# Batch 0's turns, squares and begun FFN1 pieces in another order; the last product's two column groups in one tile

## The chip, the cores and the metric

The kernel runs on one core of one Trainium2 chip. The metric is the device time of one execution in microseconds (us), as the median of several runs. One more execution is taken with the hardware profiler; its trace is where the times of single instructions come from.

A core has engines that each work through their own queue of instructions in a fixed order: TensorE (PE in the profile; its weight loads are PEld), VectorE (DVE), ScalarE (ACT), GpSimd (POOL) and SyncE (SP). They wait for each other through semaphores. Data moves between the off-chip memory and the on-chip memory by DMA transfers, which SP, ACT or POOL issue. TensorE writes its results to PSUM, eight banks of 2 KB for each of 128 partitions, and VectorE or ScalarE copy them out.

## The reference

Attention without a softmax, then a two-layer FFN with a parametric relu between the layers, on 8 batches, 12 heads, 448 positions and a head dimension of 64:

```
S = 448; scale = 1 / sqrt(64)
scores = scale * (q @ k.T)                    # per batch and head, 448 x 448
attn   = max(scores, 0) ** 2 / S
x      = (attn @ v), heads side by side       # 3584 x 768
h      = x @ w_in                             # 3584 x 2048
g      = max(h, 0) + alpha * min(h, 0)
out    = g @ w_out                            # 3584 x 768, float32
```

## The kernel before

**Work and stages.** The 12 heads of a batch form 3 groups of 4 heads, so there are 24 groups n in all; groups 0 to 2 belong to batch 0. A group's 448 positions are 64 rows (pp) by 7 columns (j), and a piece (n, j) of the scores is called a chunk here: four matmuls on quarters of the array (`score_mm`, L209), one relu over 128x896 on ScalarE or VectorE (`relu`, L218 or L220), one square (`square`, L229 or L231). After seven chunks `attnv` multiplies by v (28 matmuls, L241) and copies the result out, scaled, into xT, which is FFN1's input (L253, L255). FFN1 of a batch is 16 blocks `ff` of 128 columns, each of six matmuls over `km` (`f1_mm`, L275) and the parametric relu (`f1_out`, L281 on ScalarE and L282 on VectorE). FFN2 multiplies two token blocks at a time by w_out in seven products instead of eight (class `Pair`, L335 and L340), except for some blocks done directly (`f2`, L300). `store` (L291) sends a finished tile out in two transfers of 64 rows each.

**Turning q and k.** The scores need q and k with the head dimension on the partitions. For groups 0 to 4 TensorE does that (`turn_pe`, L183): two transposes per j into PSUM, then a copy to the tile T (L186) on VectorE or ScalarE. For the later groups a DMA transpose does it. For group 0, q is loaded in two parts in float32 and cast (`cast0`, L406), and k in two parts, j 0 to 3 and j 4 to 6.

**An order written by hand.** The order of all work is a text of words that `Walk.step` carries out one by one; each engine's queue follows from it. The words that matter here:

- `t0q24D`: group 0, q, transposes for j 2 and 3, copied by VectorE (D) or ScalarE (A). `x02D` is the cast of j 0 and 1.
- `i6`: six matmuls on an idle tile (`warm`, L165); 31 such stand at the very start.
- `cA`, `cD`: the next chunk's scores, and its relu on ScalarE or VectorE. `cAA` is two of them.
- `s1D`: the square of the chunk that is second in the list `late` of relued chunks, on VectorE.
- `v`: `attnv` of the next group; the letters behind it name the engines of the two halves of its copy (AD if none is given).
- `e4`: the next four matmuls of FFN1 pieces that are begun early: four blocks `ff`, each over `km` 0 to 3 (groups 0 and 1), 16 matmuls in all, in banks that are held. `E` completes one of them with `km` 4 and 5, once group 2 is in xT, and runs `f1_out`.
- `Lq3`, `Lv3`, `Li1`, `Lo0,0,8`: loads of q and k, of v, of w_in columns and of w_out, issued on POOL's queue in the order of the text.
- `r4e`, `r4x`, `r4y`: the last of the seven products of the last `Pair`, in two column groups (0 to 255 and 256 to 383).

The text of the first `walk` call (L502) carries batch 0's attention up to the first four FFN1 blocks. `LAST` (L514) carries the last batch's FFN. The word `z` in it makes `store` use ScalarE's queue for the second transfer of each tile, beside SP's.

**Tiles that are passed on.** The relu writes into one of six `rl` buffers, which the square reads and gives back; an instruction that needs a buffer waits for the one that reads it last. PSUM banks are handed out by `take_pair` and `take_bank`, the one longest unused first.

Of the kernel before, what the change touches and what calls it, by code (L numbers as in the profile page):

```python
# [20 lines left out]
def kernel(  # L21
# [11 lines left out]
    B, H, S, D = q.shape  # L33
# [465 lines left out]
                nc.vector.tensor_scalar(beta_sb, alpha_sb, -1.0, 1.0, ALU.mult, ALU.add)  # L499

    walk = Walk()
    walk("""Li0 Lv2 x02D x46A x24D x67A i6 t0q46D t0q24A t0q67A t0q02D t0k01D t0k24D t0k12A cA cD Lq3 cA Li1 t0k47D cA s1D t1q07D cAA s0D Li2 Lq4 s0D t1k07D cA s2D s1D Li3 cAA s0D s0D cA cDA t2q07D s1D t2k05D cA s0D Lo0,0,8 s2D Lq5 Lv3 t2k57A Lo0,8 s0D Lv4 s0D cA cA cA Lv5 s0D s0D v cA v cA s0A cD e4 e1 s0D cD s0D cA s1A s1A e5 e4 e1 s0D e1 s0D v b t3q07A t3k07D E E E E""")  # L502
    walk("""f f cADA f s0D f s1D s0D cADA f t4q07A t4k07D m o f s0D f cAAA s0D s1D d5D f f s0D f l5 Lq6 f Lq7 Lq8 g00 Lo1,0,4 s0D cADA s2D vDA cDD s3D s0D s0A g20 s0A g10 s0D cADA v s0D cAA s0D s1D s0D s0D""")
    walk("""B h h cAA h s0D s0D h v d6D l6 Lo1,4 Lv6 h E E E d7D f E f E f f d8D f l8 cAAA s1D f Lq9 f Lv7 s1A Lq10 Lv8 f f f s0D f""")
    walk.p, walk.r = Pair((0, 3), (0, 4)), Pair((0, 5), (0, 6))
# [5 lines left out]
    FIRST_PAIR = """B f s1A f s2D s0D s1D n f f s0D f f f f s0D cDA cA f s0D s1A nD pa pb r1 f pc s0A f f f f f f p6 r2 cADA s1D v cAA ra s0D pd cA p7 rb n p5 s2D p4 s0D p3 s1A s0A cADA s2A s0D rc r6 v rd cADA s2D r7 r5 s0A s0D cAAD s0A r4 r3 cA v cAA"""  # L511
    EACH = """B f s0D f s0A f n f f f f s2A f s1D cAAA s1D f f s0D f s0A f p1 nD f f r1 f f s1A pc p2 pa r2 ra pb cA vDA s1D s0D cAA p6 s0D pd p7 n cA rc s1A cAA s0D s0A p5 p4 rb p3 cAAD v cAD s1D s1A s3A cA s3A r6 s2A r7 rd r5 s0A cAD r4 s0D r3 cAD v cD cA"""
    ONE_PAIR = """B f f nD s2A s0A s2D f s1D f f f s1D f f s0A f f cAD s1D cA s0D n s0D f f f f f f pc pa g50 pb cADA v p1 cAAA s0A p6 s2D s0A p2 pd p7 s1A p5 n s0A p4 p3 s0D cADA s0D v cAD s1A s2A cD s2A s1D g51 s0D cDAD v cD cA cA"""
    LAST = """B f s0A f f f f s3A s2A s2A f f s2A f f f f f f pc f f s0A f p1 r1 pa pb p2 p6 p7 pd ra p5 rb rc p4 p3 r6 z r7 rd r5 r2 r3 r4e"""  # L514
    for b, plan in ((2, FIRST_PAIR), (3, EACH), (4, EACH), (5, ONE_PAIR), (6, EACH), (7, LAST)):
        walk.p, walk.r = ([walk.r] if b == 2 else []) + [Pair(*t) for t in pairs[b][b == 2:]] + [None] * (b == 5)
        walk(plan)
# [30 lines left out]
```

## Time and profile before

| what | value |
|---|---|
| median of 3 runs | 372.95 us (372.71, 372.95, 373.54) |
| the profiled execution, its own time | 373.66 us |
| its span, first to last instruction | 371.9 us |
| mean granted TensorE clock | 0.995 |
| VectorE, ScalarE busy | 277.9 us (75%), 274.7 us (74%) |
| chain that ended last: PE, ACT, DVE | 91%, 3%, 2% |

The span begins at 0; all places in the profile are us from there. The page gives each engine's busy time, then 40 equal slices of about 9.3 us, one digit each (9 is 90% or more busy; for PEclk, the granted share of TensorE's clock in tenths). A window's row gives the busy time of each engine in that stretch, with the number of instructions, the granted clock and the load of the DMA engines. A timeline row gives start, length, engine, line, operation, output and input, how often it follows itself, and in brackets the idle time of the engine before it and what ended it. A "released by" is inferred from semaphore events.

### The profile page before, as it was taken

The page shows a single profiled execution, that of the slowest core. Times are in us where ns is not written, and L with a number is a line of the kernel's source. Part 1 is how long each engine was busy: PE and PEld are TensorE (multiplying, and loading weights), DVE is VectorE, ACT ScalarE, POOL GpSimd, SP SyncE. Part 2 cuts the span into 40 slices and gives each one's busy share as a digit, 9 for nine tenths or more (in the row PEclk, how much of TensorE's full clock was granted, in tenths as well). Part 3 has the DMA queues.
Part 4 walks back from the last instruction along what each step waited for, and adds up shares of the span by engine and source line. Part 5 has one row for each costly group of instructions (what it writes and reads, how often), then busy time and mean ns, then how long its engine had stood idle before and what let it go on. Part 6 is the DMA issues. An engine that isn't in the chain of part 4 may idle for free.

```text
span 371.9 us, 7878 instructions
## 1 busy us (share of the span) xinstructions
PE 362.9 (98%) x3097; PEld 196.7 (53%) x3097; DVE 277.9 (75%) x445; ACT 274.7 (74%) x406; POOL 72.5 (19%) x120
## 2 busy tenths in 40 slices
PE   7799999999999999999999999999999999999996
PEld 5454564445454565545555455554555455555563
DVE  3989988885968989566887668888849667856653
ACT  4998676877997678885897859967699866964400
POOL 8567150304113222021020220202200000000000
PEclk9899999999999999999999999999999999999999
DMA  9999979998999878455882558727647201220024
GB/s 145 193 204 202 196 120 187 159 167 148 183 173 141 119 118 156 102 85 92 156 150 64 96 81 167 143 59 121 101 95 136 50 2 43 65 65 0 0 64 108
DMA packets 73557, 43.29 MB, mean 116 GB/s; under 512 B 40368, under 2 KB 73008, under 8 KB 73520
## 3 DMA queue, kind: packets, MB, share of 16 engines
q0 software_dynamic: 27136, 22.58, 42.0%
q1 hardware_dynamic: 45712, 19.61, 26.1%
q10 hardware_dynamic: 672, 0.59, 0.5%
q8 instruction: 24, 0.39, 0.4%
q14 instruction: 13, 0.11, 0.1%
HBM read 45.62 MB, written 11.01 MB: 152 GB/s over the span
## 4 chain that ended last, share of the span: by engine, by line
PE 91%; ACT 3%; DVE 2%; DMA 1%; issue 1%; ACTq 0%; DVEq 0%; POOLq 0%
PE psum L275 38%; PE psum L335 30%; PE psum L209 8%; PE psum L241 8%; PE psum L300 6%; DMA kraw<-in_k_dram 1%; ACT rl L218 1%; PE psum L183 1%; DVE gT L282 1%; ACT xT L253 1%; ACT neg L281 1%; DVE w_mix L195 1%; DVE at L231 0%; DVE T L186 0%; DVE osb L340 0%
## 5 line engine op out<-in xcount | busy, mean ns | idle before, releaser
L275 PE MATMUL psum<-xT,w_in_sb 128*128 128x448 bf16 x768 | 150.4, 353 | 0.3 <-DVE gT L282 0.2
L282 DVE SCALAR_TENSOR_TENSOR gT<-neg,beta_sb,psum 128x448 bf16<-128x448 f32 x128 | 85.2, 679 | 43.4 <-ACT neg L281 42.1
L218 ACT ACTIVATE rl<-psum 128x896 bf16<-128x896 f32 x128 | 111.1, 924 | 7.2 <-PE psum L209 5.2
L275 PEld LDWEIGHTS <-w_in_sb 128*128 128x128 bf16 x768 | 73.4, 98 | 73.2 <-issue 6.7
L281 ACT ACTIVATE neg<-psum 128x448 f32<-128x448 f32 x128 | 68.5, 547 | 41.0 <-PE psum L275 32.7
L231 DVE TENSOR_TENSOR at<-rl 128x896 bf16<-128x896 bf16 x105 | 62.1, 618 | 0.5 <-ACT rl L218 0.2
L229 ACT ACTIVATE at<-rl 128x896 bf16<-128x896 bf16 x63 | 58.5, 951 | 0.3
L335 PEld LDWEIGHTS <-S 128*128 128x128 bf16 x384 | 36.7, 98 | 28.4 <-issue 5.3
L335 PE MATMUL psum<-w_mix,S 128*128 128x384 bf16 x288 | 49.8, 326 | 0.2
L220 DVE TENSOR_SCALAR rl<-psum 128x896 bf16<-128x896 f32 x40 | 43.2, 1086 | 8.6 <-PE psum L209 8.1
L209 PE MATMUL psum<-T 64*64 64x448 bf16 x672 | 46.2, 361 | 2.1 <-DVE T L186 1.3
L418 POOL COPY landed<-T 1x1 bf16<-1x1 bf16 x18 | 4.1, 229 | 206.8 <-DMA T<-perm 183.1
L335 PEld LDWEIGHTS <-gT 128*128 128x128 bf16 x296 | 28.3, 98 | 20.2 <-issue 1.8
L241 PE MATMUL psum<-at,vraw 64*64 64x448 bf16 x672 | 36.5, 350 | 0.0
L335 PE MATMUL psum<-w_out_sb,gT 128*128 128x384 bf16 x192 | 34.0, 326 | 0.0
L340 DVE TENSOR_TENSOR osb<-psum,u 128x384 f32<-128x384 f32 (+2 forms) x37 | 20.2, 546 | 12.6 <-PE psum L335 8.2
L209 PEld LDWEIGHTS <-T 64*64 64x64 bf16 x672 | 17.4, 106 | 23.1 <-issue 14.9
L241 PEld LDWEIGHTS <-vraw 64*64 64x64 bf16 x672 | 21.2, 107 | 11.8 <-issue 2.7
L300 PE MATMUL psum<-w_out_sb,gT 128*128 128x256 bf16 (+1 forms) x128 | 22.0, 326 | 0.1
L255 DVE TENSOR_SCALAR xT<-psum 128x448 bf16<-128x448 f32 x24 | 14.9, 622 | 9.2 <-PE psum L241 8.7
L253 ACT ACTIVATE xT<-psum 128x448 bf16<-128x448 f32 x24 | 13.2, 549 | 9.1 <-PE psum L241 8.7
L356 ACT COPY osb<-psum 128x384 f32<-128x384 f32 x12 | 5.8, 479 | 17.4 <-PE psum L335 17.4
(43 smaller groups left out, 239.8 us busy)
## 6 DMA issues: line engine op xcount, KB each, us to landing
out_dram<-osb SPq DMA_DIRECT2D x91, 96.0 KB, 2.3
vraw<-in_v_dram POOLq DMA_DIRECT2D x24, 224.0 KB, 6.6
qraw<-in_q_dram POOLq DMA_DIRECT2D x23, 224.0 KB, 4.1
kraw<-in_k_dram POOLq DMA_DIRECT2D x23, 224.0 KB, 5.3
w_in_sb<-in_moe_w_in_dram POOLq DMA_DIRECT2D x16, 192.0 KB, 8.1
w_out_sb<-in_moe_w_out_dram POOLq DMA_DIRECT2D x4, 512.0 KB, 10.5
w_out_sb<-in_moe_w_out_dram POOLq DMA_DIRECT2D x4, 256.0 KB, 8.8
out_dram<-osb SPq DMA_DIRECT2D x8, 128.0 KB, 3.6
```

The lines of the kernel that those rows point to most:

```text
L209: nc.tensor.matmul(ps[64 * c:64 * c + 64, r, :S], t[64 * r:64 * r + 64, 1, j, 64 * c:64 * c + 64], t[64 * r:64 * r + 64, 0, :, 64 * c:64 * ...
L218: nc.scalar.activation(rl, ps[:, :, :S], ACTF.Relu)
L220: nc.vector.tensor_scalar(rl, ps[:, :, :S], 0.0, None, ALU.max)
L229: nc.scalar.activation(a, rl, ACTF.Square)
L231: nc.vector.tensor_tensor(a, rl, rl, ALU.mult)
L241: nc.tensor.matmul(ps[64 * s:64 * s + 64, r, :S], vv[64 * r:64 * r + 64, s, j, :], a[64 * r:64 * r + 64, s], start=(j == 0), stop=(j == NJ ...
L275: nc.tensor.matmul(ps, w_in_sb[:, km // 2, km % 2, bass.ts(ff, 128)], xT[b][:, km // 2, km % 2, :], start=(km == 0), stop=(km == KM - 1))
L281: nc.scalar.activation(neg, ps, ACTF.Relu, scale=-1.0)
L282: nc.vector.scalar_tensor_tensor(gT[:, ff, (b % 2) * S:(b % 2) * S + S], neg, beta_sb[:, ff:ff + 1], ps, ALU.mult, ALU.add)
L300: nc.tensor.matmul(ps, gT[:, ff, bass.ts(c, 128)], w_out_sb[:, ff, first_col + lo:first_col + hi], start=(ff == 0), stop=(ff == KF - 1))
L335: nc.tensor.matmul(ps, left[:, i], right[:, i], start=(start and i == 0), stop=(i == KH - 1), skip_group_check=not start)
L340: nc.vector.tensor_tensor(t, ps, u, ALU.add)
```

## The change

Two texts change; no function does. All of the rest of the order is the same.

```diff
-    walk("""Li0 Lv2 x02D x46A x24D x67A i6 t0q46D t0q24A t0q67A t0q02D t0k01D t0k24D t0k12A cA cD Lq3 cA Li1 t0k47D cA s1D t1q07D cAA s0D Li2 Lq4 s0D t1k07D cA s2D s1D Li3 cAA s0D s0D cA cDA t2q07D s1D t2k05D cA s0D Lo0,0,8 s2D Lq5 Lv3 t2k57A Lo0,8 s0D Lv4 s0D cA cA cA Lv5 s0D s0D v cA v cA s0A cD e4 e1 s0D cD s0D cA s1A s1A e5 e4 e1 s0D e1 s0D v b t3q07A t3k07D E E E E""")
+    walk("""Li0 Lv2 x02D x46A x24D x67A t0q24D t0q02D i6 t0q46D t0q67D t0k01A t0k12D t0k24D Lq3 cD cA t0k47D Li1 cA s1D Li2 s0D t1q07D cA cA cA Lq4 t1k07D s1D Li3 s1D cA s0D s1D cA cA s0D t2q07D cA s1D cD cA t2k05D s2D s0D Lo0,0,8 Lq5 Lv3 Lo0,8 cA t2k57A Lv4 s1D s0D Lv5 cA cA s0D cA s0D vDA cA v cA cD s0A e1 e4 s0D cA cD e1 s1A s0D e6 e2 s1A e2 s0D s0D vDA b t3q07A t3k07D E E E E""")
...
-    LAST = """B f s0A f f f f s3A s2A s2A f f s2A f f f f f f pc f f s0A f p1 r1 pa pb p2 p6 p7 pd ra p5 rb rc p4 p3 r6 z r7 rd r5 r2 r3 r4e"""
+    LAST = """B f s0A f f f f s3A s2A s2A f f s2A f f f f f f pc f f s0A f p1 r1 pa pb p2 p6 p7 pd ra p5 rb rc p4 p3 r6 z r7 rd r5 r2 r3 r4x r4y"""
```

On the engines this means, in batch 0's part:

- TensorE: eight of group 0's fourteen q transposes stand ahead of the six idle matmuls; after the first part of k only two chunks' scores come ahead of the rest of k, not three; group 1's k is turned after group 0's last chunks, not among them; the 16 early FFN1 matmuls come in other portions.
- ScalarE: ahead of its first relu one T copy remains of three; relus and squares of batch 0 are 17 and 3 in both.
- VectorE: two more T copies (128x256 and 128x128 in size) ahead of its first relu; that relu is chunk 0's now and was chunk 1's; 4 relus and 18 squares in both.
- POOL: the same instructions in the same order.

At the end, `r4e` called `p4` with two column groups, each with its own osb tile and its own `store` (two transfers of 64 rows each, one on SP and one on ScalarE). `r4x r4y` call these two methods, which were in the kernel before and not used:

```
def p4x(self, lo=0, hi=256):
    if lo == 0:
        self.o4 = o_pool.tile([128, d_model - CUT], F32, tag="o", name="osb")[:, :NH]
    y = take_bank()[:, :hi - lo]
    self.mm(y, self.a22, w_mix[3][:, :, lo:hi], True)
    self.plus(y, self.u3[:, lo:hi], self.o4[:, lo:hi])
    if hi == NH:
        store(*self.b, 0, NH, self.o4)

def p4y(self):
    self.p4x(256, NH)
```

The matmuls and the two adds on VectorE are the same; the transfers are one pair of 64 rows by 384 columns instead of one pair by 256 and one by 128.

## The prediction

> **What bounds the kernel now.** I began with the page's engine row and its slices.
>
> ```profile
> PE 362.9 (98%) x3097; PEld 196.7 (53%) x3097; DVE 277.9 (75%) x445; ACT 274.7 (74%) x406; POOL 72.5 (19%) x120
> PE   7799999999999999999999999999999999999996
> PEclk9899999999999999999999999999999999999999
> ```
>
> TensorE is full from the third slice to the last. Work that only moves between ScalarE and VectorE can pay in the first two slices (0 to about 19 us) or in the last one, and nowhere else. The second PEclk digit is an 8, so I cut that stretch into equal windows (columns: stretch, its length, then busy time with instruction count for each engine, PEclk, DMA share, GB/s).
>
> ```profile
> 3.87:7.28 3.41, 2.09 (x43) 1.50 (x44) 1.67 (x6) 1.41 (x5) 3.41 (x6) 1.00 1.43 150
> 7.28:10.70 3.42, 2.95 (x62) 1.51 (x52) 3.03 (x6) 3.33 (x5) 2.93 (x6) 1.00 1.24 193
> 10.70:14.11 3.41, 1.51 (x24) 0.80 (x26) 3.41 (x7) 3.41 (x6) 2.06 (x3) 1.00 1.20 192
> 14.11:17.52 3.41, 3.41 (x48) 2.19 (x51) 3.22 (x6) 2.98 (x5) 1.88 (x3) 0.50 1.22 187
> 17.52:20.94 3.42, 3.33 (x73) 1.95 (x65) 3.12 (x7) 3.42 (x6) 1.63 (x3) 1.00 1.26 203
> ```
>
> From 7.3 to 14.1 us ScalarE and VectorE are full (3.33 to 3.41 of 3.41) and TensorE is not: the relus and squares bound this stretch. After the window in which TensorE is least busy (1.51 of 3.41, 44%) its clock is granted at 0.50 for one window, and there TensorE becomes the bound (3.41 of 3.41). Next, ScalarE's timeline.
>
> ```profile
> 6.83 0.27 ACT L186 COPY T<-psum 128x128 bf16<-128x128 bf16 x1 [0.70 <-PE psum L183]
> 7.37 8.21 ACT L218 ACTIVATE rl<-psum 128x896 bf16<-128x896 f32 x10 [0.28 <-PE psum L209]
> 16.01 0.92 ACT L218 ACTIVATE rl<-psum 128x896 bf16<-128x896 f32 x1 [0.43 <-PE psum L209]
> ```
>
> Ten relus in 8.21 us without a gap: with a mean of 0.95 (neighbours overlap) a new one starts every (8.21 - 0.95) / 9 = 0.81 us. Then ScalarE waits 0.43 us for TensorE, inside the half-speed window. Ahead of the first relu ScalarE is mostly idle: k's first part lands only then, as TensorE's timeline says.
>
> ```profile
> 6.37 0.41 PE L183 MATMUL psum<-ident,kraw 128*64 128x128 bf16 x8 [0.66 <-DMA kraw<-in_k_dram]
> 6.94 0.78 PE L209 MATMUL psum<-T 64*64 64x448 bf16 x12 [0.15 <-DVE T L186]
> 8.34 0.38 PE L209 MATMUL psum<-T 64*64 64x448 bf16 x4 [0.34 <-ACT rl L218]
> 9.17 0.57 PE L209 MATMUL psum<-T 64*64 64x448 bf16 x8
> 11.75 1.03 PE L209 MATMUL psum<-T 64*64 64x448 bf16 x16 [1.18 <-DVE T L186]
> ```
>
> The last line is the hole that empties the 44% window: 1.18 us behind VectorE's copy of head group 1's turned k. For the end I read the transfers: KB each and us from issue to landing.
>
> ```profile
> out_dram<-osb SPq DMA_DIRECT2D x91, 96.0 KB, 2.3
> out_dram<-osb ACTq DMA_DIRECT2D x3, 96.0 KB, 2.4
> out_dram<-osb ACTq DMA_DIRECT2D x1, 32.0 KB, 1.9
> ```
>
> **The change, part by part.** The base is the profiled execution: 373.66 us, span 371.9. It lies 0.71 above the median of the runs shown (372.95); those runs are 372.71, 372.95 and 373.54.
>
> *1. q's turns and copies (L183, L186).* Two of ScalarE's copies (128x256, about 0.37, and one 128x128, 0.27) go to VectorE, and eight of the fourteen q transposes stand ahead of the six idle matmuls. All of it ends before k lands: VectorE's casts end at 4.87 (4.19 + 0.68), the fourteen transposes need 0.58 us and the six idle matmuls some 0.4, so TensorE is done at about 5.9 and VectorE's fourth q copy at about 6.3; k's first transpose starts at 6.37. Cost 0. The cover is the wait for k (0.66 us on TensorE, 0.70 idle on ScalarE); without it VectorE's extra 0.5 us would count. For the same reason the 0.64 us taken off ScalarE gains nothing: they stood ahead of a ScalarE that waited anyway.
>
> *2. The first two chunks change engines.* k's first copy goes from VectorE (about 0.22) to ScalarE (0.27): +0.05 ahead of the first score. Chunk 0's relu goes to VectorE and ScalarE takes chunk 1, which is ready four matmuls later: 0.57 - 0.38 = 0.19 (rows of 8 and 4 matmuls). ScalarE's first relu starts at 7.37 + 0.05 + 0.19 = 7.61, 0.24 later. VectorE's starts 0.2 earlier.
>
> *3. The same lists to the end of group 2.* From the first relu to group 2's last square ScalarE has in both orders 17 relus, 3 squares, two xT evictions and one copy; VectorE 4 relus and 18 squares. The queue is full, so 0.24 goes through unless a wait goes away. One does, in ScalarE's timeline:
>
> ```profile
> 21.92 1.04 ACT L229 ACTIVATE at<-rl 128x896 bf16<-128x896 bf16 x1
> 22.99 0.92 ACT L218 ACTIVATE rl<-psum 128x896 bf16<-128x896 f32 x1
> ```
>
> The relu at 22.99 waits for the square in front of it to end (21.92 + 1.04 = 22.96), where a step of about 0.8 gives 22.75; in the new order it waits for VectorE's work instead, long done: -0.2. One comes: VectorE's last relu of group 2 now waits for a ScalarE square to return its rl buffer. It starts at 22.69 (VectorE's timeline), while that square (21.92, now 22.1 at the least) ends at about 23.1: up to +0.4 on VectorE, with three squares queued behind it, and TensorE's last attention product waits for those. At the first FFN1 completion (27.07) this sums to between 0 (the two waits of ScalarE cancel) and +0.4 (VectorE's wait passes through whole). I take +0.15, on the low side, because that product runs through the earlier operands while it waits for the last. The changed FFN1 pieces are the same 16 matmuls at 0.19 us, moved inside stretches in which TensorE waits for operands: 0; with that cover gone each costs its 0.19.
>
> *4. The clock.* In the new order k of group 1 is turned after three more chunks of group 0, so the 1.18 us hole is gone and scores come at ScalarE's pace. In 10.70 to 14.11 that is four chunks of 0.38, and the k turn of 0.58, less about 0.1 of overlap: 2.0 of 3.41 us, 58%. The window of 2.09 (61%) kept its full clock, that of 1.51 lost it; 2.0 lies next to the first. In 3.87 to 7.28 I count 0.4 of idle matmuls, 1.0 of q turns with the six others, 0.4 of k and 0.3 of scores: 2.1, as before. So I expect no half-speed window. What it cost: ScalarE's eleventh relu could have started at 7.37 + 10 x 0.81 = 15.44 and started at 16.01, 0.57 late; half the window, 1.71, is the most. I take 0.70, near the row, about the size by which the profiled run exceeds the median. Lower bound of the gain 0, if the window comes elsewhere.
>
> The Trainium skill (TensorE: Matmul & The Clock Gate, Part 1: The HAM clock gate) says that the clock falls back after an idle window of about 3.4 us, and that the windows run free of the kernel's start. The row shows a fall after a window that was 44% busy, so "idle" is not to be taken literally here; taken so, there would be no window to lose, and the sum would be 373.66 + 0.16 = 373.8. Free-running windows would let one execution of this kernel have the slow window and another not; no run here shows that, since only the profiled one has its clock.
>
> *5. Later loads.* The POOL queue has the same instructions in the same order, with the DMA engines full (share 1.2), so landings stay. With TensorE some 0.5 us earlier the closest user is the first FFN2 product at 45.62 (16 matmuls in 1.91, so 0.11 each): it reaches w_out's last four row blocks after twelve, at 46.9, and their transfer, issued at 35.93, lands after at most 9.4, at 45.4. That leaves 1.5 us of room: 0.
>
> *6. The tail.* Before: VectorE ends the 256 columns at 368.19 and the 128 columns at 368.50; each group leaves by two transfers, and ScalarE's last is issued at 369.01, behind its first (the row below): 369.01 + 1.9 = 370.9.
>
> ```profile
> 368.22 0.69 ACTq L291 DMA_DIRECT2D out_dram<-osb  x1
> ```
>
> After: nothing leaves until 368.50, then SP and ScalarE issue at about 368.53 at once: SP 368.53 + 2.1 to 2.3, ScalarE 368.53 + 2.4 = 370.9. The issue that is saved is paid back by the larger transfer: +0.01. Bounds: -0.48 (it lands like the 32 KB row, 1.9) and +0.2 (like an SP landing of 2.3, with ScalarE's usual 0.3 behind it). VectorE's second add waits for no more than now, and fewer osb buffers are in use.
>
> Sum: 373.66 - 0.70 + 0.15 + 0.01 = 373.1 us. Against the median that is +0.15, no change: 0.2% (0.75 us) is about what a measurement of this kernel can tell from none.
>
> **Rivals.** *The half-speed window stays or moves* (slower). Place: the window after 14.1, or the one after 7.3 if 3.87 to 7.28 falls short. Price: 0.70 again. It decides once a window's TensorE share drops from 2.0 toward 1.5 of 3.41; nothing in the rows says where between lies the edge. 373.1 + 0.7 = 373.8, with up to 0.4 more if the window after 7.3 is hit, where 2.95 us of work would need 5.9 in 3.41. For it: the runs at 373.54 and 373.66. Against: the evener pace of scores.
>
> *The tail does gain*: the last landing follows the number of transfers, not their size: 373.1 - 0.48 = 372.6. For it: four transfers in flight at once before. Against: the 96 KB pair on ScalarE's queue takes 2.4 wherever it stands.
>
> *ScalarE's relief counts*: the 0.64 us of copies were on the path: 373.1 - 0.64 = 372.5. Against: the idle 0.70 and 0.28 right behind them. Only together with the gain of the tail (372.0), or if part 3 comes out better than its lower end too, does this pass 372.2.
>
> **How the numbers follow.** Forecast 0.52; half-speed window 0.25; tail 0.10; relief 0.06; both of these 0.07. Faster by over 0.2% (under 372.20) needs two gains at once, or one and luck elsewhere: 0.13. Slower (over 373.70) is most of the clock rival, the rest of which stays just under: 0.22. Within: 0.65. The range reaches from 372.2, where the single gains with their own spread end, to 374.1 (373.8 plus most of the 0.4): about 0.13 and 0.07 are left out.
>
> **What would show it.** Clock record: 1.00 throughout from 3.87 on, about 2.0 of 3.41 busy in 10.7 to 14.1. ScalarE's first relu near 7.6, and no 0.43 wait near 16. TensorE's first FFN1 completion near 26.5 instead of 27.07. The last two issues at 368 less about 0.5, landing 2.1 to 2.4 later. It is wrong if a 0.50 row stands anywhere after 3.87, if ScalarE's relus have gaps, if TensorE has fallen behind or waits at FFN1 for w_in, or if the last landing is under 2.2 us after its issue.

## The result, and the profile after

| | before | after |
|---|---|---|
| median | 373.15 us (372.64 to 373.88, 20 runs) | 373.94 us (373.45 to 375.61, 20 runs) |
| ratio to before | | 1.0024, 95% interval 1.0014 to 1.0035 |
| the profiled execution | 373.66, span 371.9, clock 0.995 | 373.67, span 371.5, clock 1.00 |
| median of the time less the span | 1.80 (112 runs of all comparisons) | 2.16 (20 runs) |

The change costs some 0.8 us, between 0.14 and 0.35 per cent. The two profiled executions seem to say that nothing happened (373.66 and 373.67), but the one of before had a half-speed window, and the one of after has a span 0.4 us shorter with the same time: the difference lies outside the span, where no row of a profile stands.

The same windows as before, of the changed kernel (stretch, length, busy time and count for each engine, PEclk, DMA share, GB/s):

```profile
3.87:7.28 3.41, 2.82 (x49) 1.70 (x46) 2.16 (x9) 1.01 (x4) 3.41 (x6) 1.00 1.40 149
7.28:10.70 3.42, 2.54 (x52) 1.42 (x48) 2.70 (x6) 3.42 (x5) 2.63 (x5) 1.00 1.24 191
10.70:14.11 3.41, 2.19 (x40) 1.00 (x36) 3.41 (x7) 3.41 (x5) 1.65 (x4) 1.00 1.25 201
14.11:17.52 3.41, 2.52 (x50) 1.56 (x50) 3.41 (x7) 3.30 (x6) 2.58 (x4) 1.00 1.18 186
17.52:20.94 3.42, 3.42 (x63) 1.86 (x56) 3.37 (x7) 3.42 (x6) 1.79 (x3) 1.00 1.26 203
```

In this execution TensorE is at full clock throughout and busy 2.19 of 3.41 us where it was 1.51. ScalarE and VectorE in the changed kernel (start, length, operation, idle time before it and what ended it):

```profile
6.20 0.27 ACT L186 COPY T<-psum 128x128 bf16<-128x128 bf16 x1 [1.08 <-PE psum L183]
7.14 9.02 ACT L218 ACTIVATE rl<-psum 128x896 bf16<-128x896 f32 x11 [0.68 <-PE psum L209]
```

```profile
6.95 1.09 DVE L220 TENSOR_SCALAR rl<-psum 128x896 bf16<-128x896 f32 x1 [0.28 <-PE psum L209]
...
10.63 0.62 DVE L186 COPY T<-psum 128x896 bf16<-128x896 bf16 x1 [0.72 <-PE psum L183]
11.17 2.76 DVE L231 TENSOR_TENSOR at<-rl 128x896 bf16<-128x896 bf16 x5
```

ScalarE's first relu starts at 7.14. That is earlier than before's 7.37 only because k's first part landed at 5.87 and not at 6.33: counted from that landing it is 1.27 us, not 1.04. VectorE waits 0.72 for the turned k of group 1, which landed at 9.96. TensorE's first FFN1 completion is at 26.60 (before 27.07, forecast 26.5), its last matmul starts 340.87 us later (before 340.88). The 0.47 by which the first completion came earlier is no gain of the order: from k's landing it is 20.73, and 20.74 before, with the half-speed window in between. At the end:

```profile
367.05 1.46 SPq L291 DMA_DIRECT2D out_dram<-osb  x2
367.05 1.49 ACTq L291 DMA_DIRECT2D out_dram<-osb  x2
367.28 0.74 DVE L340 TENSOR_TENSOR osb<-psum,u 128x256 f32<-128x256 f32 x2 [0.26 <-PE psum L335]
```

VectorE's last add ends at 367.28 + 0.74 = 368.02, the last two transfers are issued at 368.04 and 368.05, and the last lands at 370.43, 2.41 us after VectorE's end (before: 368.50, 370.92, 2.42).

### The profile page after: what moved, and what is told of

Read it like the earlier page. It is cut to its first block, busy times and chain, and to the rows that moved or that the text cites. A ratio compares the mean times of both kernels' runs of the same rounds, so it can differ in the third digit from the quotient of the medians.

```text
span 371.5 us, 7872 instructions
## 1 busy us (share of the span) xinstructions
PE 362.6 (98%) x3097; PEld 195.9 (53%) x3097; DVE 278.2 (75%) x447; ACT 273.9 (74%) x404; POOL 71.5 (19%) x120
## 4 chain that ended last, share of the span: by engine, by line
PE 91%; DVE 3%; DMA 2%; ACT 1%; POOL 1%; issue 1%; POOLq 0%; ACTq 0%
PE psum L275 38%; PE psum L335 30%; PE psum L241 9%; PE psum L209 9%; PE psum L300 6%; DMA kraw<-in_k_dram 2%; DVE gT L282 1%; DVE at L231 1%; ACT xT L253 1%; PE psum L183 1%; ACT neg L281 1%; DVE w_mix L195 1%; POOL kraw L148 0%; DVE T L186 0%; DVE rl L220 0%
## 5 line engine op out<-in xcount | busy, mean ns | idle before, releaser
L418 POOL COPY landed<-T 1x1 bf16<-1x1 bf16 x18 | 3.2, 177 | 205.8 <-DMA T<-perm 182.6
L300 PE MATMUL psum<-w_out_sb,gT 128*128 128x256 bf16 (+1 forms) x128 | 22.0, 326 | 0.1
```

What stands on the lines that cost most here:

```text
L300: nc.tensor.matmul(ps, gT[:, ff, bass.ts(c, 128)], w_out_sb[:, ff, first_col + lo:first_col + hi], start=(ff == 0), stop=(ff == KF - 1))
```

## The experiments

All medians come with those of the kernel before on the same chip: 373.01 for the first four, 373.07 for the next four, 373.04 for the next three, 373.34 for the last. A ratio can differ from the quotient of two medians by about a thousandth; the ratio and its interval count. Three quantities are read of every execution: its time, its span, and its mean clock; a clock of 0.995 is one half-speed window (3.41 x 0.5 of 371 us), while 0.998 and 0.999 come from the end of the span, where the record stands at one half after the last matmul (in the profile of the kernel with beta on ScalarE from 369.97 on). "Landing to E" is the time from the landing of k's first part to the first FFN1 completion in the profiled execution.

**The two kernels again, and each half of the change alone.** `e_front` has only the first text, `e_tail` only the second:

```diff
-    ... r5 r2 r3 r4e"""
+    ... r5 r2 r3 r4x r4y"""
```

> The kernel before, unchanged, as a control. Both theories: ratio 1.000 within 0.1%. What it adds is the span of each run. Theory A (the changed order itself costs time between the first and the last instruction): the time outside the span is the same 2.1 to 2.2 us as in the changed kernel's runs. Theory B (part of the loss lies outside the span, ahead of the first instruction): outside the span it shows about 1.8 us in every run, as its one profiled execution does (373.66 - 371.9).

> The changed kernel again, on the same chip as the others of this call: ratio 1.002 (1.001 to 1.0035). Both theories: the same. It gives a second trace: if k of head group 1 lands again more than 3.5 us after k's first part (2.87 in the trace of before, 4.10 in that of after), the late landing belongs to the change; if near 2.9, it is chance.

> Only the first text changed (batch 0), the tail as before. Theory A: all of the loss is here, ratio 1.002 to 1.003, and outside the span as in the kernel before. Theory B: about half of it is outside the span, so either 1.001 with 1.8 us outside, or 1.002 with 2.2 us outside if it is this text that shifts the program. A third theory, that the tail loses: 1.000.

> Only the last product's two column groups in one tile, two transfers instead of four; batch 0 as before. My prediction's part 6: 0.0 us (ratio 1.000), last landing at the same distance from VectorE's last add (2.42 us). Theory B: 1.000 with 1.8 us outside, or 1.001 with 2.2 us outside. Third theory (the tail loses): 1.002.

| | median | ratio to before | lowest span | time less span |
|---|---|---|---|---|
| before again | 373.40 | 0.9999 (0.9978 to 1.0019) | 370.9 | 1.78 |
| after again | 374.45 | 1.0041 (1.0023 to 1.0058) | 371.6 | 2.13 |
| order alone | 373.46 | 1.0016 (1.0005 to 1.0027) | 371.4 | 1.78 |
| end alone | 373.79 | 1.0021 (1.0008 to 1.0033) | 371.0 | 2.14 |

Both halves lose, in different places: the order inside the span (lowest 371.4 against 370.9), the end outside it (2.14 against 1.80) with the span of before. Half of the 8 runs of after again had a half-speed window, its profiled one too, which is part of why its median is the highest. In that profile k of group 1 landed 4.39 us after k's first part. By what was expected this would belong to the change, but with the old order it came 2.87 to 4.68 after and with the new one 2.92 to 4.39 (most of them in the table further down): it scatters from execution to execution.

**What makes the time outside?** Two kernels with before's order and the changed end: one lets ScalarE's queue take over a store earlier, the other sends the one tile by four transfers.

```diff
-    ... rc p4 p3 r6 z r7 rd r5 r2 r3 r4e"""
+    ... rc p4 z p3 r6 r7 rd r5 r2 r3 r4x r4y"""
```

```diff
-                store(*self.b, 0, NH, self.o4)
+                store(*self.b, 0, 256, self.o4[:, :256])
+                store(*self.b, 256, NH, self.o4[:, 256:])
```

> Before's order of batch 0, the end as changed (one tile, two transfers), and ScalarE's queue takes over one store earlier, so that it issues as many output transfers as before the change while SP issues two fewer. What is asked: the time of a run less its span, 1.80 us with the four transfers at the end and 2.14 with the two. Theory 1 (it follows how many transfers ScalarE's queue carries): back to about 1.8, and the time about 0.3 below that of the changed end alone (ratio to before about 1.001). Theory 2 (it follows SP's number, or all transfers together): stays at 2.1, ratio about 1.002. Theory 3 (it was the chance of a chip or an execution): values that scatter between. Inside the span all expect no change (371.6).

> Before's order of batch 0; at the end both column groups in one tile after the second add, as changed, but sent by four transfers (256 columns, then 128), as many as before. Theory 1 (the number of transfers sets the time after the last instruction): time less span back to about 1.8. Theory 2 (the tile, or that the last two transfers start together, sets it): 2.1. Inside the span both expect the last landing later than with two transfers, since each queue issues its second pair some 0.3 to 0.5 us behind its first: the last landing 2.3 to 2.6 us after VectorE's end instead of 2.4, so the span 0 to 0.2 longer.

Medians 373.51 (ratio 1.0012, 0.9999 to 1.0025) and 373.82 (1.0024, 1.0004 to 1.0044); time less span 2.15 and 2.14. So neither the number of transfers nor the queue that carries them matters outside the span: four transfers give 2.14 like two. Inside it, the four land last at 370.19, 2.44 us after VectorE's end of 367.75: also no difference.

All kernels with 2.1 have one thing in common that none with 1.8 has. Counting every instruction in VectorE's program, waits and branches too (the page's count leaves them out), it is 570 instructions long, not 571 (the traces record two fewer in each program, 568 and 569): the second add writes into a tile that is already held, and so needs no instruction of its own to wait for the tile's earlier transfers. Three kernels test that alone. One adds a tiny memset to the changed end, near 1 us where VectorE is idle; one adds it to the kernel before; one takes an instruction off VectorE in the kernel before, far from the end.

```diff
     nc.vector.memset(idle, 1.0)
+    nc.vector.memset(beta_sb, 0.0)
```

```diff
-                nc.vector.tensor_scalar(beta_sb, alpha_sb, -1.0, 1.0, ALU.mult, ALU.add)
+                nc.scalar.activation(beta_sb, alpha_sb, ACTF.Copy, scale=-1.0, bias=1.0)
```

> The changed end alone (before's order of batch 0), and one more tiny memset on VectorE near 1 us, where VectorE is idle. The four kernels with the changed end have 2.14 us outside the span whatever their transfers, the ones without it 1.80; the one instruction count that splits them is VectorE's: 570 against 571, since the add into the shared tile needs one wait instruction less. Theory A (the number of instructions in VectorE's program decides the time after the last instruction): with 571 again, time less span back to 1.80 and the time to some 373.4 (0.35 less than the changed end alone). Rival B (the wait for the two old transfers, which the last add no longer makes, or the shared tile, decides): stays at 2.14.

> The kernel before with that one tiny memset on VectorE and nothing else: VectorE 572 instructions. Theory A, if each instruction less costs 0.35: 1.45 outside the span and 372.7; if it is a matter of even and odd or of an edge between 570 and 571: 2.14 or 1.80. Rival B: 1.80 and no change of the time. Inside the span all expect 0.

> The kernel before with beta (128x16, 0.17 us, near 27 us) computed on ScalarE in place of VectorE: VectorE 570 instructions, the end untouched with its four transfers, two tiles and all its waits. Theory A: time less span 2.14, the time 0.35 above before, though nothing at the end has changed. Rival B: 1.80. Inside the span 0 to +0.2 (ScalarE's first neg of FFN1 stands behind it).

| | VectorE's instructions | last output | median | ratio | time less span |
|---|---|---|---|---|---|
| changed end, memset | 571 | two transfers | 373.04 | 1.0003 (0.9989 to 1.0016) | 1.76 |
| before, memset | 572 | four | 373.46 | 1.0011 (0.9997 to 1.0025) | 1.86 |
| before, beta on ScalarE | 570 | four | 373.71 | 1.0011 (0.9997 to 1.0025) | 2.16 |

Theory A holds and rival B falls: with 571 instructions the changed end is back at the time of before; with 570 the kernel before, whose end is untouched, has the 2.16. The ratios of the last two do not separate from 1 by themselves (a third of their 12 runs had a half-speed window), the time outside the span does, run by run: over all comparisons it was 1.73 to 1.86 in the 184 runs of programs with 571, and 2.08 to 2.21 in the 76 with 570. "0.35 for each instruction less" falls too, since 572 gives 1.86: it is a step between 570 and 571. Whether the 0.36 lies ahead of the first instruction or behind the last, no run tells.

**What makes the order slower?** Two kernels with the new order and the old end: the first two chunks with their old engines, and group 1's k turned two squares later.

```diff
-    ... t0k01A t0k12D t0k24D Lq3 cD cA t0k47D ...
+    ... t0k01D t0k24D t0k12A cA cD Lq3 t0k47D ...
```

```diff
-    ... Lq4 t1k07D s1D Li3 s1D cA ...
+    ... Lq4 s1D Li3 s1D t1k07D cA ...
```

> The new order of batch 0 with the old end, but the first two chunks keep the engines they had before: k's first copy on VectorE, chunk 0's relu on ScalarE, chunk 1's on VectorE. The theory of the prediction (part 2: the change of engines starts ScalarE 0.24 us late, and its queue is full): ScalarE's first relu 1.05 us after k's first part lands instead of 1.28, and the first FFN1 completion some 0.2 us earlier after that landing than in the new order alone (20.50), so about 20.3. The rival (the later turn of group 1's k, or the waits for rl buffers, sets it): the same 20.5, with the 0.2 us lost in a wait further on. Time less span 1.8 in both.

> The new order of batch 0 with the old end, but the turn of group 1's k stands two squares later in VectorE's and TensorE's order. The theory to be tested: the new order is the slower for putting VectorE's copy of that k ahead of squares, so that a late landing of it (3.5 to 4.4 us after the first k) holds VectorE up. Then no wait of VectorE for TensorE in front of that copy, and the first FFN1 completion 20.4 to 20.5 us after the first k's landing even if group 1's k lands more than 3.5 after it (20.7 to 21.0 in the changed kernel). The rival (the scores of group 1 are needed that early): ScalarE's relus wait for scores where they did not, and the completion is at 20.7 or later.

| | median | ratio | lowest span | runs with a half-speed window |
|---|---|---|---|---|
| old engines | 373.43 | 1.0009 (0.9995 to 1.0024) | 370.9 | 4 of 12 |
| k of group 1 later | 373.55 | 1.0012 (0.9990 to 1.0034) | 371.6 | 10 of 12 |

With the old engines the lowest span is again that of before, but the first relu came 1.18 us after the landing, not the expected 1.05:

```profile
6.61 0.57 PE L209 MATMUL psum<-T 64*64 64x448 bf16 x8 [0.29 <-DVE T L186]
7.04 1.73 ACT L218 ACTIVATE rl<-psum 128x896 bf16<-128x896 f32 x2 [0.42 <-PE psum L209]
```

The relu follows the first score by 0.43, as in before (6.94 and 7.37); with the new engines it is 0.62 (6.52 and 7.14 in the changed kernel). So about 0.2 us of the delay is ScalarE's wait for the second chunk. The rest stands ahead of the first score, 0.75 after the landing here, 0.65 in the changed kernel and 0.61 in before: in this execution TensorE was at half speed until 5.32, q's transposes ended at 6.0 only, and VectorE's copies of q stand ahead of k's in the new order. The expected 20.3 from landing to E can't be read: a half-speed window lies in between. Among the runs without such a window the median span hardly moves, though: 371.5 in the two kernels with the new order and the old engines (16 runs, the kernel with both repairs below among them), 371.6 with the new engines (25 runs), 371.2 with the old order (157 runs). So the old engines bring back the lowest spans, and that the engines are the whole cost of the order is not shown; how much the copies of q cost was not tried alone.

The later k is no repair: it had a half-speed window in 10 of 12 runs, the profiled one too, and with it 21.05 us from landing to E, not the expected 20.4 to 20.5. Its windows show it:

```profile
8.97:12.39 3.42, 1.85 (x32) 0.86 (x33) 3.35 (x7) 3.36 (x5) 1.95 (x4) 1.00 1.25 199
12.39:15.80 3.41, 3.41 (x42) 1.80 (x44) 3.32 (x6) 3.20 (x4) 1.96 (x4) 0.50 1.20 190
```

The theory behind it, that the new order suffers more from a late k of group 1, finds no support in the following table, of the profiled executions without a half-speed window before E (only one of the new order has a late landing):

| order | kernel | k of group 1 lands after k's first part | first relu after that landing | from first relu to E |
|---|---|---|---|---|
| old | before, beta on ScalarE | 2.98 | 1.05 | 19.16 |
| old | changed end, four transfers | 3.43 | 1.05 | 19.16 |
| old | before again | 3.57 | 1.12 | 19.23 |
| old | changed end | 3.66 | 1.05 | 19.16 |
| old | before, memset | 3.73 | 1.12 | 19.34 |
| old | changed end, memset | 4.05 | 1.07 | 19.41 |
| old | changed end, earlier store | 4.68 | 1.22 | 19.92 |
| new | order alone | 2.92 | 1.35 | 19.16 |
| new | old engines and memset (below) | 3.35 | 1.21 | 19.16 |
| new | after | 4.10 | 1.27 | 19.46 |

The first relu and E in the order alone, then in the kernel before with beta on ScalarE:

```profile
7.58 9.01 ACT L218 ACTIVATE rl<-psum 128x896 bf16<-128x896 f32 x11 [0.68 <-PE psum L209]
26.73 2.44 PE L275 MATMUL psum<-xT,w_in_sb 128*128 128x448 bf16 x12
```

```profile
7.33 9.02 ACT L218 ACTIVATE rl<-psum 128x896 bf16<-128x896 f32 x11 [0.28 <-PE psum L209]
26.49 2.82 PE L275 MATMUL psum<-xT,w_in_sb 128*128 128x448 bf16 x14
```

From ScalarE's first relu to E both orders need the same 19.16 us, and both lose 0.1 to 0.8 where group 1's k landed late. What differs is the first relu.

**Both repairs in the changed kernel**: the old engines for the first two chunks, and the memset.

> The changed kernel with two repairs: the first two chunks keep their old engines, and the tiny memset brings VectorE's program back to 571 instructions. If the loss of the changed kernel is those two things (0.37 us outside the span by the instruction count, 0.2 to 0.4 inside it by the engines of the first chunks), the time is that of before: time less span 1.79, lowest spans 370.9 to 371.1 (371.3 in the changed kernel), median 373.0 to 373.4, ratio to before 0.999 to 1.001. If the other reordering of batch 0 costs too, or the parts add up to more than their sum, the lowest spans stay at 371.3 and the median is 373.5 or more.

Median 373.56 against 373.34, ratio 1.0013 (0.9997 to 1.0029); time less span 1.79 as expected, lowest span 371.0, within 0.1 of before's 370.9. The lowest span is what the repairs were expected to give; the median is not (373.0 to 373.4 was expected, 373.5 or more if the rest of the order costs too). That the loss inside the span is gone is therefore not shown: the ratio's interval holds both 0 and a quarter of a per cent, 4 of the 12 runs had a half-speed window, and the kernel before, run as its own control, had a median of 373.40 in 12 runs against 373.01 in 31. No version tried beats the kernel before. The profiled execution with both repairs shows one more thing, a late landing far behind batch 0's part (with the memset, lines stand one further down: L301 is L300):

```profile
45.08 1.47 PE L301 MATMUL psum<-w_out_sb,gT 128*128 128x256 bf16 x12
47.20 0.60 PE L301 MATMUL psum<-w_out_sb,gT 128*128 128x256 bf16 x4 [0.65 <-DMA w_out_sb<-in_moe_w_out_dram]
```

w_out's last part landed at 47.16, 10.9 us after its issue (8.8 to 9.6 in the thirteen other traces), and TensorE waited for it.

## Why the prediction came out as it did

Forecast 373.1, 0.15 over the median of the 3 runs then known; measured 373.94, 0.79 over the median of 20. That lies inside the range (372.2 to 374.1), but partly by luck: the range reaches that high for a half-speed window that stays, and nearly half of the loss came from where no part of the sum looked, outside the span.

*Part 1 (q's turns hidden): right, with a cover that runs out at times.* In the changed kernel k's transposes wait 0.17 us for the landing, not for q:

```profile
5.91 0.41 PE L183 MATMUL psum<-ident,kraw 128*64 128x128 bf16 x8 [0.17 <-DMA kraw<-in_k_dram]
```

In the profile of the order alone, where TensorE came to full speed at 6.87 only, q's transposes end no sooner than k lands, and k follows them without a wait:

```profile
5.91 0.53 PE L183 MATMUL psum<-ident,qraw 128*64 128x128 bf16 x6
6.27 0.64 PE L183 MATMUL psum<-ident,kraw 128*64 128x128 bf16 x8
6.95 0.57 PE L209 MATMUL psum<-T 64*64 64x448 bf16 x8
```

The first relu stands 1.35 after the landing there, 0.08 more than in the changed kernel.

*Part 2 (ScalarE starts 0.24 later): right.* 1.27 against 1.05, 0.22, of which 0.19 is the wait for the second chunk (0.62 against 0.43 behind the first score). The spans of runs without a half-speed window agree: median 371.2 before (93 runs), 371.5 after (13 runs).

*Part 3 (+0.15, which holds part 2's 0.24 too): the two waits were named rightly and summed a little low.* VectorE's timeline of the order alone has the new wait, where the old order (second fence, the kernel before with beta on ScalarE) has none:

```profile
22.66 1.09 DVE L220 TENSOR_SCALAR rl<-psum 128x896 bf16<-128x896 f32 x1 [0.30 <-ACT at L229]
23.66 1.69 DVE L231 TENSOR_TENSOR at<-rl 128x896 bf16<-128x896 bf16 x3
```

```profile
22.12 1.08 DVE L220 TENSOR_SCALAR rl<-psum 128x896 bf16<-128x896 f32 x1
23.12 1.69 DVE L231 TENSOR_TENSOR at<-rl 128x896 bf16<-128x896 bf16 x3
```

Counted from the first relu (7.58 and 7.33), VectorE's last three squares end at 17.77 in the new order and 17.48 in the old. ScalarE has the reverse; its last squares in the new order, then in the old:

```profile
23.10 1.99 ACT L229 ACTIVATE at<-rl 128x896 bf16<-128x896 bf16 x2
```

```profile
23.22 1.78 ACT L229 ACTIVATE at<-rl 128x896 bf16<-128x896 bf16 x2
```

They end at 17.51 and 17.67. The last operand is ready at 17.77 (VectorE's) in the one and 17.67 (ScalarE's) in the other: the wait went from one engine to the other, and E doesn't move (19.16). So the two waits together give nothing, and part 2's 0.22 goes through: 0.22 where the sum had +0.15, between its bounds of 0 and +0.4.

*Part 4 (the clock, -0.70): wrong, and the step that failed most.* It took the half-speed window of the profiled execution for a property of the order. Most executions of before don't have it: 39 of 196 with the old order had one (mean clock under 0.9965), and 23 of 64 with the new one (the kernel with the later k left out). The prediction named the possibility in its paragraph on free-running windows and still took the 0.70 off. The hole of 1.18 us doesn't decide it: the kernel before with beta on ScalarE has it too, and there the window's edge at 11.57 cuts it (2.22 and 2.42 busy), and no drop follows:

```profile
11.71 0.57 PE L209 MATMUL psum<-T 64*64 64x448 bf16 x8 [1.18 <-DVE T L186]
```

So the median never held the 0.70; subtracting it only brought the base of 373.66 down to the median, and the new order has the window more often. A window costs 372.6 - 371.5 = 1.1 us in the new order and 371.9 - 371.2 = 0.7 in the old (medians of spans with and without it), so on average some 0.36 x 1.1 - 0.20 x 0.7 = 0.25 us more, an estimate. The rule of the share (a full clock kept at 2.0, lost near 1.5) fell as well. Windows before a drop, cut at the clock's own edges, were busy 1.51, 1.83, 1.85 and 2.28 of 3.41 us; the least busy windows of the other traces, with no drop behind them, 1.86 to 2.31. This is the 2.28, in the kernel with the old engines:

```profile
12.14:15.56 3.42, 2.28 (x40) 1.16 (x34) 3.42 (x7) 3.42 (x5) 1.89 (x3) 1.00 1.24 202
15.56:18.97 3.41, 3.41 (x40) 1.75 (x43) 3.41 (x7) 3.20 (x5) 2.05 (x4) 0.50 1.21 194
```

What decides a drop, and why the new order has it more often (by these counts), stays open. That windows run free of the kernel's start, which the Trainium skill says (TensorE: Matmul & The Clock Gate, Part 1: The HAM clock gate) and which the prediction could not see, is borne out: full speed began anywhere from 3.87 to 7.04 us in the fourteen profiles, though the first matmul starts at 1.06 in all of them. (A window's clock column says 1.00 ahead of that too, where there is no record; the transposes tell: k's eight took 0.64 us in the order alone, partly at half speed, and 0.41 in before.)

*Part 5 (later loads, 0): right for the usual execution.* The last w_out part was issued at 36.77 and landed at 46.04, against 35.93 and 45.36; with TensorE at that product from 45.15, and twelve matmuls at the 0.12 that its row shows (1.91 us for 16) before it is needed, the room was 0.5 us rather than 1.5. One slow landing used it up in another kernel, as shown.

*Part 6 (the tail, +0.01): right inside the span*: 2.41 against 2.42 us from VectorE's end to the last landing. What it missed lies outside the span: 0.36 us, through one instruction less on VectorE. No part of the prediction asked what the change does to the time outside the span; it carried that difference over as a constant.

The sum by what was measured: 0.36 outside, 0.22 from parts 2 and 3, some 0.25 from the clock, together 0.8. The median spans agree: 371.8 after and 371.3 before, 0.5 apart.

*The rivals.* The half-speed window did stay, in some executions and not in others, and by the estimate above accounts for about a third. The tail's gain didn't come. ScalarE's relief counted for nothing: it waits 1.08 and 0.68 us ahead of its first relu.

## What to carry to other kernels

Before a state seen in one profiled execution (a slow window, a late landing) goes into a sum, look how many of the timed runs have it: their clock and span tell, and the median may not contain it. At differences of a thousandth, compare time and span for each run separately; a change can act outside the span, and then an instruction that does no work is the right control. When an order is changed around full engines, count from the first full instruction to the next join: here both orders took 19.16 us, and only the start had moved.

## What was not expected of the hardware

The time outside the span changes by a step with the length of VectorE's program: 2.15 us (2.08 to 2.21) with 570 instructions, 1.79 (1.73 to 1.86) with 571, 1.86 (1.82 to 1.90) with 572. The numbers of instructions on ScalarE (654 to 658) and SP (233 to 236) don't go with it. In the traces the final barrier ends alike with 570, 571 and 572: VectorE's last record starts 0.006 to 0.007 us after ScalarE's, and TensorE's ends last, 0.03 us after VectorE's. What happens behind it or ahead of the first instruction, and where other steps lie, wasn't tried.
